# Reading two PSUM banks behind the sums that run beside them, and loading q further ahead in pieces

## The chip, the cores and the metric

The kernel runs on one core of one Trainium2 chip. The metric is the device time of one execution in microseconds (us), inputs and outputs in the chip's main memory. The span: first to last instruction; a kernel's trace is of one of its timed executions, that of the kernel before of a further one, of 982.29 us. The granted clock is the share of its full clock that the trace records for TensorE (PE in the profile): 1.00, or 0.5 in what is called half-clock stretches below. In this kernel TensorE multiplies matrices, VectorE (DVE) adds and multiplies elementwise, ScalarE (ACT) copies and does activations, SyncE (SP) issues transfers.

## The reference, cut to what matters

```python
def _attn_ref(q, k, v, g_norm):                    # (8, 8, 576, 64)
    kv = np.einsum('bhsd,bhse->bhde', k, v)
    out = np.einsum('bhsd,bhde->bhse', q, kv)
    rms = np.sqrt(np.mean(out * out, axis=-1, keepdims=True) + 1e-06)
    return out / rms * g_norm

def _moe_ref(x, w_in, w_out, s, b):                # x: 4608 x 512, w_in: 512 x 2048
    h = x @ w_in
    r = np.maximum(h, 0.0)
    g = s * (r * r) + b
    return g @ w_out                               # w_out: 2048 x 512
```

## The kernel before

The 4608 tokens are 36 chunks of 128, four chunks to a unit, so units 0 to 8. In each unit a first half computes h and g (`mm1`), a second half multiplies by w_out (`mm2`). Both replace eight products by seven and some sums (Strassen's scheme); from unit 2 on, five of the seven products with w_out are cut once more in the same way (`second_level`). So TensorE runs products while VectorE runs the sums for the products that come next. Attention for the next unit is mixed into the first half. In the trace of the kernel before, sums that were ready stood for 2.44 us behind a read that was not and that is written before them. So the order below sets here what waits for what.

The part of a second half (unit 2 and later) that the change touches:

```python
        def x5_of(j):                                   # the S1 T1 product
            st["x", j] = half(("x", j), "x")            # a PSUM bank
            product(5, j, st["x", j], True)             # 8 matmuls of 256 columns (16 in the profile)
            scaled(right("o2", j), st["x", j], b_21)    # VectorE reads the bank
        ...
            p2[5]()
            pump(2)                                     # two of w_out's tiles are loaded
            x5_of(0)
            s2((2, 3))                                  # sums in SBUF
            p6["sums"]((5, 6))
            p2[3]()
            p2[4]()
            pump(2)
            at(1)                                       # attention work, in unit 2 alone
            x5_of(1)
            p6["sums"]((7, 3))
            p7["sums"]((5, 6, 7))
            at(2)
            pump(2)
            p6[1]()                                     # product into the t bank, then VectorE reads it
            s4((0,))
            p6[2]()
            p6[6]()                                     # next product into the same t bank
```

The S1 T1 product is one of the seven, of a sum made from g and a sum made from w_out. `w_out`'s tiles stand in a ring of seven. The result of `x5_of`, in `right("o2", j)`, is not used until near the end of the unit. q is loaded two chunks at a time into one of two buffers, in short rows:

```python
            for h in range(H):
                for a in range(2):
                    rows = slice(32 * (2 * (h % 2) + a), 32 * (2 * (h % 2) + a) + 32)
                    nc.sync.dma_start(
                        out=to[rows, h // 2, w : w + n, :],
                        in_=src[h, :, j : j + n, a * 32 : a * 32 + 32],
                    )
```

That is 16 transfers for each run of positions of one batch. Most pairs of chunks are one such run; some are two (32 transfers) and one is three (48).

## Time and profile before

| | before |
|---|---|
| time of 3 runs, median (range) | 986.51 us (984.99 to 988.79) |
| the profiled run | 982.29 us, span 980.5 us |
| TensorE busy | 945.9 us, 96% |
| TensorE waiting for VectorE's read of the t_ps bank | 16.5 us, in seven waits |
| half-clock stretches after those waits | 5, of 3.413 us each |
| mean granted clock | 0.990 |

An engine that is busy for 96% of the span leaves little to win by waiting less; the table's last two rows show that waiting can also cost clock: five of the seven waits were followed by 3.413 us at 0.50.

### The profile page before, as it was taken

To read this page: it belongs to the slowest core of one execution; us is meant where nothing else is said; L and a number is where in the kernel's file an instruction comes from. 1 tells how busy PE (TensorE), PEld (TensorE's weight loads), DVE (VectorE), ACT (ScalarE), POOL (GpSimd) and SP (SyncE) were. 2 spreads that over 40 slices of the span, in tenths; PEclk is the share of its full clock that TensorE was granted. 3 is DMA by queue.
4 is the path that set the end of the run, shared out by engine and by line. 5 is a ranking of instruction groups with operands and counts; after the bars stand their busy time and mean duration, and the time that the engine had idled before them with its cause. 6 is when DMAs were issued, how large, how long until landed. Compare 5 with 4: busy or idle time off the path is not lost.

```text
span 980.5 us, 17772 instructions
## 1 busy us (share of the span) xinstructions
PE 945.9 (96%) x7270; PEld 846.2 (86%) x7270; DVE 641.9 (65%) x1167; ACT 192.8 (20%) x366; POOL 6.7 (1%) x18
## 2 busy tenths in 40 slices
PE   7999999999999899999999999999999999999997
PEld 6888888888888898889879888988898988898987
DVE  2789666584467666766477756766676667664674
ACT  3683132102121023200320023101320022001100
POOL 2000000000000000000000000000000000000000
PEclk9999999999999999999999999999999999999999
DMA  9679736497653546155445554355435530553054
GB/s 247 216 282 260 251 80 176 131 297 232 182 121 119 194 133 193 41 194 171 140 110 171 187 177 110 121 194 172 120 90 195 187 99 18 196 170 123 25 200 140
DMA packets 136656, 158.46 MB, mean 162 GB/s; under 512 B 77696, under 2 KB 91776, under 8 KB 136448
## 3 DMA queue, kind: packets, MB, share of 16 engines
q1 hardware_dynamic: 133472, 155.57, 52.3%
q10 hardware_dynamic: 2784, 1.77, 0.8%
q8 instruction: 57, 0.93, 0.4%
q14 instruction: 23, 0.19, 0.1%
q0 software_dynamic: 320, 0.00, 0.0%
HBM read 131.34 MB, written 25.95 MB: 160 GB/s over the span
## 4 chain that ended last, share of the span: by engine, by line
PE 87%; DVE 5%; DMA 4%; ACT 2%; SPq 1%; issue 1%; DVEq 0%; ACTq 0%
PE x_ps L91 39%; PE y_ps L91 26%; PE z_ps L91 9%; PE t_ps L91 8%; PE x_ps L434 3%; DVE sub L245 2%; PE kv_ps L372 2%; DMA w_sb<-w 1%; SPq L167 1%; DMA w_raw<-in_moe_w_in_dram 1%; DMA kv_sb<-in_k_dram 1%; ACT xT L484 1%; DVE o L697 1%; DVE sub L242 0%; DVE xT L478 0%
## 5 line engine op out<-in xcount | busy, mean ns | idle before, releaser
L582 ACT COPY r<-x_ps 128x512 f32<-128x512 f32 x96 | 56.3, 586 | 435.3 <-PE x_ps L91 393.6
L91 PE MATMUL y_ps<-xs,wb 128*128 128x256 f32 x512 | 122.7, 382 | 0.0
L91 PE MATMUL x_ps<-xs,ws 128*128 128x256 f32 x512 | 121.5, 380 | 0.0
L91 PEld LDWEIGHTS x_ps<-xs,ws 128*128 128x128 f32 x512 | 96.9, 190 | 14.0 <-issue 1.0
L91 PEld LDWEIGHTS y_ps<-xs,wb 128*128 128x128 f32 x512 | 95.3, 190 | 14.6 <-issue 2.2
L91 PE MATMUL x_ps<-xT,wa 128*128 128x256 f32 x384 | 90.3, 381 | 0.1
L242 DVE TENSOR_TENSOR a<-y_ps,r 128x512 f32<-128x512 f32 x64 | 44.1, 689 | 66.8 <-ACT r L582 61.9
L91 PEld LDWEIGHTS x_ps<-xT,wa 128*128 128x128 f32 x384 | 71.8, 190 | 11.1 <-issue 1.2
L91 PE MATMUL x_ps<-w_sb,a 128*128 128x256 f32 (+1 forms) x376 | 79.7, 364 | 0.0
L91 PE MATMUL t_ps<-w_sb,sub 128*128 128x128 f32 x448 | 63.1, 302 | 16.5 <-DVE r L697 16.5
L91 PEld LDWEIGHTS t_ps<-w_sb,sub 128*128 128x128 f32 x448 | 60.4, 215 | 18.2 <-DVE r L697 17.8
L91 PEld LDWEIGHTS x_ps<-w_sb,a 128*128 128x128 f32 x376 | 66.9, 190 | 8.4 <-issue 0.6
L537 DVE SCALAR_TENSOR_TENSOR a<-a 128x512 f32<-128x512 f32 x96 | 66.4, 691 | 3.1
L91 PE MATMUL y_ps<-w_sb,sub 128*128 128x128 f32 x504 | 62.0, 275 | 0.0
L91 PE MATMUL x_ps<-xT,ws 128*128 128x256 f32 x256 | 60.9, 381 | 0.5
L91 PEld LDWEIGHTS y_ps<-w_sb,sub 128*128 128x128 f32 x504 | 60.2, 192 | 0.7
L91 PE MATMUL z_ps<-xT,wa 128*128 128x256 f32 x256 | 60.5, 379 | 0.0
L91 PE MATMUL x_ps<-w_sb,s 128*128 128x256 f32 x256 | 57.8, 380 | 0.0
L91 PEld LDWEIGHTS x_ps<-xT,ws 128*128 128x128 f32 x256 | 47.8, 190 | 8.2 <-ACT r L582 2.1
L91 PEld LDWEIGHTS z_ps<-xT,wa 128*128 128x128 f32 x256 | 48.6, 190 | 6.6
L91 PE MATMUL y_ps<-w_sb,a 128*128 128x128 f32 (+1 forms) x360 | 54.3, 300 | 0.0
L91 PEld LDWEIGHTS x_ps<-w_sb,s 128*128 128x128 f32 x256 | 47.5, 190 | 6.0 <-issue 0.2
(139 smaller groups left out, 1236.4 us busy)
## 6 DMA issues: line engine op xcount, KB each, us to landing
w_sb<-w SPq DMA_DIRECT2D x147, 512.0 KB, 4.6
w_sb<-w SPq DMA_DIRECT2D x35, 256.0 KB, 2.8
w_raw<-in_moe_w_in_dram SPq DMA_DIRECT2D x8, 1024.0 KB, 8.1
w_raw<-in_moe_w_out_dram SPq DMA_DIRECT2D x8, 1024.0 KB, 5.3
w_sb<-in_k_dram SPq DMA_DIRECT2D x48, 144.0 KB, 2.9
w_sb<-in_v_dram SPq DMA_DIRECT2D x48, 144.0 KB, 3.0
out_dram<-o SPq DMA_DIRECT2D x104, 64.0 KB, 2.4
w<-sub SPq DMA_DIRECT2D x20, 256.0 KB, 3.9
```

Of the source, the lines that this page charges most:

```text
L91: nc.tensor.matmul(o, lhsT=lhsT, rhs=rhs, start=start, stop=stop, skip_group_check=True)
L167: nc.sync.dma_start(out=to[rows, h // 2, w : w + n, :], in_=src[h, :, j : j + n, a * 32 : a * 32 + 32],)
L242: nc.vector.tensor_tensor(out=o, in0=a, in1=b, op=ALU.add)
L245: nc.vector.tensor_tensor(out=o, in0=a, in1=b, op=ALU.subtract)
L372: nc.tensor.matmul(ps[r][l * HB : l * HB + HB, i, :], lhsT=kv[l][rows, 0, j, :], rhs=kv[l][rows, 1, j, :], start=(j == 0), stop=(j == R - 1),)
L434: nc.tensor.matmul(ps[32 * p : 32 * p + 32, w, :], lhsT=st["qT"][:, p, 32 * w : 32 * w + 32], rhs=bd_kv[(b if w < 2 else b1) % 2][:, p, :] ...
L484: nc.scalar.activation(to[:, i], to[:, i], AF.Copy, scale=g_col[:, i : i + 1])
L537: nc.vector.scalar_tensor_tensor(t, t, 0.0, t, ALU.max, ALU.mult)
L582: nc.scalar.copy(st[name], src)
L697: nc.vector.scalar_tensor_tensor(o, ps, s_col, other, ALU.mult, ALU.add)
```

## The change

Two things. First, the reads of the two x_ps banks are put behind sums that are ready earlier, so that VectorE works while TensorE is at the product, and then reads. Second, q of a unit's second pair of chunks is issued one unit earlier, in eight pieces between w_out's tiles, in place of one run at a unit's start. The arithmetic is the same. The core of the diff (the moves of attention work inside unit 2 that follow from it, and unit 1's loads, are cut):

```diff
-        def x5_of(j):
+        def x5_of(j, *between):
             st["x", j] = half(("x", j), "x")
             product(5, j, st["x", j], True)
+            for fn in between:
+                fn()
             scaled(right("o2", j), st["x", j], b_21)
 ...
-            x5_of(0)
-            s2((2, 3))
-            p6["sums"]((5, 6))
+            at(("q", 2))
+            x5_of(0, lambda: s2((2, 3)), lambda: p6["sums"]((5, 6)))
             p2[3]()
             p2[4]()
             pump(2)
+            at(("q", 3))
             at(1)
-            x5_of(1)
-            p6["sums"]((7, 3))
-            p7["sums"]((5, 6, 7))
+            x5_of(1, lambda: p6["sums"]((7, 3)), lambda: p7["sums"]((5, 6, 7)))
 ...
+    def loads_in_parts(u, i, parts):
+        left = []
+        def part(n):
+            if n == 0 and u < U:
+                left.extend(load_q(4 * u + 2 * i))
+            k = -(-len(left) // (parts - n))
+            for load in left[:k]:
+                load()
+            del left[:k]
+        return [partial(part, n) for n in range(parts)]
 ...
+        for n, fn in enumerate(loads_in_parts(u + 2, 1, 8)):
+            second["q", n + 2] = [fn]
 ...
-            loads(u + 1, 0 if u < 3 else 1)
+            if u < 3:
+                loads(u + 1, u - 1)
```

More of the change, by code (lines that the diff above doesn't have):

```diff
@@ L158, in load_q @@
                 q_in[R] = t[:, DM:].rearrange("p (a w) -> p a w", a=NP)
+        rest = []
         for w, b, j, n in pieces:
@@ L166, in load_q @@
                     rows = slice(32 * (2 * (h % 2) + a), 32 * (2 * (h % 2) + a) + 32)
-                    nc.sync.dma_start(
-                        out=to[rows, h // 2, w : w + n, :],
-                        in_=src[h, :, j : j + n, a * 32 : a * 32 + 32],
+                    rest.append(
+                        partial(
+                            nc.sync.dma_start,
+                            out=to[rows, h // 2, w : w + n, :],
+                            in_=src[h, :, j : j + n, a * 32 : a * 32 + 32],
+                        )
                     )
+        return rest
     wide = moe_w_in.dtype != FP32
@@ L974, in rest @@
             pump(2)
+            at(("q", 0))
             step["x3"]()
@@ L980, in rest @@
             pump(2)
+            at(("q", 1))
             at(0)
@@ L996, in rest @@
             pump(2)
+            at(("q", 3))
             at(1)
-            x5_of(1)
-            p6["sums"]((7, 3))
-            p7["sums"]((5, 6, 7))
+            x5_of(1, lambda: p6["sums"]((7, 3)), lambda: p7["sums"]((5, 6, 7)))
             at(2)
             pump(2)
+            at(("q", 4))
             p6[1]()
@@ L1011, in rest @@
             pump(2)
+            at(("q", 5))
             st["r2"] = rp.tile([P, 2, HN], FP32, name="or2", tag="rb")
@@ L1017, in rest @@
             pump(2)
+            at(("q", 6))
             p7[2]()
@@ L1022, in rest @@
             pump(2)
+            at(("q", 7))
             at(3)
@@ L1030, in between @@
                 pump(2)
+                at(("q", 8))
                 p4[1]()
@@ L1043, in rest @@
             pump(4)
+            at(("q", 9))
             y4_of(0, 3)
@@ L1046, in rest @@
             pump(2)
+            at(("q", 10))
         return {"sums": p1["sums"], "rest": rest}
@@ L1182, in side_of @@
             }
+        if u == 1:
+            for n, fn in enumerate(loads_in_parts(3, 0, 8)):
+                side.setdefault(6 + n, []).append(fn)
         return side
@@ L1187, in loads @@
         if u < U:
-            load_q(4 * u + 2 * i)
+            for load in load_q(4 * u + 2 * i):
+                load()
[6 more added lines that the diff above has]
+            for load in left[:k]:
+                load()
+            del left[:k]
+        return [partial(part, n) for n in range(parts)]
     tile_at = {1: 3, 2: 4, 3: 5, 4: 6, 5: 7, 6: 8, 7: 9, 9: 10, 10: 11, 11: 12, 12: 13, 14: 14, 15: 15}
@@ L1221, in sides @@
             first[1, 2] = [lambda: kv_product(kv_due[u]), lambda: pump(NP)]
-        first.setdefault((1, 2), []).append(lambda: loads(*((u + 1, 1) if u < 3 else (u + 2, 0))))
+        place, half = ((1, 2), (u + 2, 0)) if u > 2 else (((1, 2), (2, 1)), ((2, 2), (4, 0)))[u - 1]
+        first.setdefault(place, []).append(lambda: loads(*half))
         if u == 1 or u + 1 == U:
@@ L1226, in sides @@
         for s in range(NS):
-            j = s if u > 2 else s - 2
+            j = s if u > 2 else s - 1
             if j >= 0:
@@ L1232, in sides @@
         if u == 2:
-            first[3, 1].append(lambda: loads(4, 0))
-            second = {
-                0: [turn[2], product[2]], 1: [norm[2]], 2: [turn_x[2], turn[3]],
-                3: [product[3]], 4: [norm[3], turn_x[3]],
-            }
+            second = {0: [turn[3], product[3]], 1: [norm[3]], 2: [turn_x[3]]}
+        for n, fn in enumerate(loads_in_parts(u + 2, 1, 8)):
+            second["q", n + 2] = [fn]
         second[5] = [lambda: [sums() for sums in x_sums(u + 1)]]
```

## The prediction

> **What bounds the kernel now.** I read the page first, then the waits of TensorE, then its stream of instructions around one wait, then the granted clock around all of them, and last the wait on q.
>
> The page says that TensorE is the bound, and which wait it has in the steady state:
>
> ```profile
> PE 945.9 (96%) x7270; PEld 846.2 (86%) x7270; DVE 641.9 (65%) x1167; ACT 192.8 (20%) x366; POOL 6.7 (1%) x18
> ...
> L91 PE MATMUL t_ps<-w_sb,sub 128*128 128x128 f32 x448 | 63.1, 302 | 16.5 <-DVE r L697 16.5
> ```
>
> TensorE is busy for 96% of the span, so only what it waits for, or runs slowly for, can be won without taking matmuls away. The view of waits, for TensorE alone, begins:
>
> ```profile
> PE t_ps L91 <- DVE r L697: 16.5, 7, 3.4
> PE x_ps L434 <- DVE qT L404: 4.4, 3, 2.3
> ```
>
> Seven waits for VectorE's read of t_ps, 16.5 us together, and three for a transposed q, 4.4 us together. Unit 0 and 1 do not run this part, units 2 to 8 do: seven units, one wait each (3.37 us in unit 2, 2.18 or 2.19 in the others). The stream of VectorE and TensorE around the wait of unit 3 shows its cause:
>
> ```profile
> 424.71 0.48 DVE L697 SCALAR_TENSOR_TENSOR o<-x_ps,s_col,b 128x256 f32<-128x256 f32 x1 [2.44 <-PE x_ps L91]
> ...
> 426.29 3.62 PE L91 MATMUL x_ps<-w_sb,s 128*128 128x256 f32 x16
> ...
> 429.95 0.48 DVE L697 SCALAR_TENSOR_TENSOR o<-x_ps,s_col,b 128x256 f32<-128x256 f32 x1 [1.58 <-PE x_ps L91]
> ...
> 432.88 0.68 DVE L245 TENSOR_TENSOR sub<-a 128x512 f32<-128x512 f32 x1
> 433.48 0.34 DVE L697 SCALAR_TENSOR_TENSOR r<-t_ps,s_col,o 128x128 f32<-128x128 f32 x1
> ...
> 433.88 4.57 PE L91 MATMUL t_ps<-w_sb,sub 128*128 128x128 f32 x24 [2.19 <-DVE r L697]
> ```
>
> The reads of the x_ps bank (o<-x_ps, the S1 T1 product) stand ahead of sums that do not need it. VectorE sits idle 2.44 and then 1.58 us for the two products to end, and does its sums afterwards. Five of them (430.35 to 433.48) stand between the second read and the read of t_ps, and TensorE's next product into t_ps may not start before that read.
>
> There is a second cost, which no wait shows: the 24 matmuls after the wait take 4.57 us in unit 3 and 2.94 in unit 4. A table of 12 us around each wait has the granted clock in the column after POOL (here units 3, 4, 5 and 8):
>
> ```profile
> 430.69:442.69 12.00, 9.81 (x73) 9.62 (x73) 8.07 (x18) 0.00 (x0) 0.00 (x0) 0.86 0.47 163
> 538.52:550.52 12.00, 9.82 (x87) 9.63 (x87) 8.41 (x19) 0.00 (x0) 0.00 (x0) 1.00 0.59 196
> 642.32:654.32 12.00, 9.82 (x73) 9.63 (x73) 8.06 (x18) 0.00 (x0) 0.00 (x0) 0.86 0.49 172
> ...
> 947.59:959.59 12.00, 9.82 (x88) 9.63 (x88) 8.40 (x19) 0.00 (x0) 0.00 (x0) 1.00 0.58 198
> ```
>
> Five of seven waits (units 2, 3, 5, 6 and 7) are followed by a stretch at half clock: 0.86 of 12 us is 3.4 us at one half. Last, the longest wait for q, in unit 4, in the chain that ended last:
>
> ```profile
> 490.75 1.61 DMA q_sb<-in_q_dram
> ...
> 492.54 0.72 DVE qT L404
> ...
> 493.39 1.08 PE x_ps L434 x32
> ```
>
> The q tile of that pair of chunks is cut into 48 transfers, which the sync queue issues in one run from 474.5 to 498.8 us; the 32nd lands at 492.36, VectorE transposes, TensorE has waited 2.34 us.
>
> [...] the starts of the slow stretches, 328.61, 434.43, 646.05, 751.87 and 854.27 us, lie whole multiples of 3.413 apart. [...] On that grid, windows with 2.05 to 2.19 us of waiting were followed by half clock, and windows with 1.46 us (unit 4) or 1.58 us (the q wait at 306 us) were not. So where a wait of 2.18 us falls on the grid decides whether it costs 1.65 us more.
> [...] ready sums stand behind a read that waits 2.44 us. [...] one issue takes the sync queue 0.44 us (median of 304), 48 take over 20.
>
> **The change, part by part.** No matmul, sum or byte is added or removed; order alone moves.
>
> (1) The first read of x_ps goes behind two s2 sums and two p6 sums, the second behind five sums. Replayed for unit 3 with the starts above (a sum takes 0.60 to 0.72 us start to start): VectorE is free at 422.2; four sums, 2.53 us, end at 424.7, when the first x_ps is ready (424.71 before as well); read until 425.1; the two y_ps reads wait for TensorE, the last is done at about 426.7; five sums, 3.13 us, end at about 429.9; x_ps is ready at 429.95, read until 430.35; t_ps's first product ends at 430.64, its read runs from 430.84 to about 431.15. TensorE asks for t_ps at about 431.6. The wait is gone, by a margin of some 0.4 us. Six units (3 to 8): 6 × 2.18 = 13.1 us.
> Unit 2 carries attention work too. Its replay: y_ps reads done at 318.95, the norm's two instructions 0.9, five sums 3.13, read 0.4, transpose of xn 0.63, so t_ps is read from about 324.0 to 324.3, and TensorE asks at 323.9. It keeps about 0.5 of 3.37 us: 2.9 saved. (It had another transpose of q there, 0.6 us, which the change moves to the first half.)
>
> (2) Without those waits there is no window with 2 us idle: five half-clock stretches go. Each costs 4.57 − 2.94 = 1.63 us (in unit 2, 1.33 + 0.34 = 1.67). 5 × 1.65 = 8.2 us.
>
> (3) q of the second half is issued in eight pieces during the previous unit's second half, up to 60 us ahead of use. The 2.34 us wait of unit 4 goes. The one at 306 us (1.58) stays: q had landed long before, its transpose stands behind VectorE's sums, and the new order keeps that place. The 0.46 and 0.54 us waits of earlier units stay.
>
> Sum: 13.1 + 2.9 + 8.2 + 2.3 = 26.5 us, or 2.7%.
>
> **The rivals.**
> - A wait takes the place of the one removed: the read of t_ps is still late because the sums end late, or the x_ps bank is freed late. Against it: the replay's margin is 0.4 us, and each x_ps bank is next written by a product some 15 us on. If a wait of about 1 us stayed in seven units, 7 us would come back: about 965.
> - The sync queue becomes the bound: q pieces sit in front of w_out's tiles, and TensorE waits for w_sb. For it: around unit 1's end the queue has hardly a pause from 225 to 254 us, and the change puts 28 issues of 0.48 us (13 us) in there. I replayed that queue issue by issue: it is 9 us late at 252 us, the first 16 transfers of unit 2's q are issued by 241, the other 16 by 263, and are wanted near 256 and 269. Nothing waits, but the second margin is only some 5 us. Against it in units 3 to 8: the queue spends most of the second half waiting for TensorE to free a slot, and a piece costs 0.9 us (2.6 in the unit with 48). A miss in unit 2 would cost up to 6 us and one slow stretch: about 965.
> - q was hidden anyway, and part (3) gives nothing: 2.3 us less, about 960.
> - The half-clock stretches stay, set off by other waits: 8 us less, about 966. Against it: the 1.58 us wait set none off.
>
> **Range and chances.** The profiled run took 982.3 us, the timed ones 985.0, 986.5 and 988.8. Taking 26.5 off gives 956 from the profiled run and 960 from the median. The timed runs' surplus may be more half-clock stretches (the three waits of over 2 us that tripped none in the profile would add 3 × 1.65 = 5 us), and those would go too. I choose 958. A miss of one rival brings 965; everything at once and all timed surplus gone, 953. So 952 to 966. Faster by over 2% means under 966.8: 0.86. Within 2%: 0.13. Slower needs a new wait of over 46 us, which nothing here suggests: 0.01.
>
> **What would show it.** Right: TensorE's waits for t_ps vanish in units 3 to 8 and fall to about 0.5 us in unit 2; VectorE's idle time of 2.44 and 1.58 us before the reads of x_ps falls to under 0.3; the granted clock is 1.00 in all seven stretches, with 24 t_ps matmuls at 2.94 us; the wait for q in unit 4 is gone and that of 1.58 us in unit 2 is still there; units 3 to 7 each take about 101.7 us. Wrong: a wait of TensorE for w_sb or q in unit 2, a t_ps wait of 1 us or more, slow stretches elsewhere. If the waits go and the time falls by less than 20 us, TensorE has found another wait that I did not name.

## More of the kernel before

One line that the prediction tells but does not show is the sync queue's stream in the first half of unit 4: start, duration, and the 48 issues for one pair of chunks between two lots of w_out's tiles.

```profile
474.54 24.23 SPq L167 DMA_DIRECT2D q_sb<-in_q_dram  x48
498.87 1.41 SPq L666 DMA_DIRECT2D w_sb<-w  x3
```

## The result, and the profile after

| | before | after |
|---|---|---|
| median of 6 runs (range) | 986.56 us (984.9 to 989.54) | 957.9 us (956.88 to 959.2) |
| ratio | | 0.9706, 95% interval 0.9687 to 0.9725 |
| the profiled run, span | 980.5 us | 955.3 us |
| mean granted clock, profiled run | 0.990 | 0.999 |
| t_ps waits of TensorE | 16.5 us, 7 | 0.4 us, 1 |
| waits for a transposed q | 4.4 us, 3 | 2.1 us, 2 |
| waits for w_out's tiles (w_sb) | none | 1.9 us, 2 |
| half-clock stretches, but for the kernel's end | 5 | 0 |

Ratios here are the mean time of one kernel's fast runs over that of the other's fast runs in the same rounds, so not quite the ratio of the medians. All outputs are right.

The page of the changed kernel, to be held against the two lines shown of before; the group of t_ps matmuls has gone from 302 ns each to 275, and from 16.5 us idle to 0.4:

```profile
PE 938.2 (98%) x7270; PEld 838.4 (88%) x7270; DVE 643.9 (67%) x1167; ACT 192.3 (20%) x366; POOL 6.7 (1%) x18
...
L91 PE MATMUL t_ps<-w_sb,sub 128*128 128x128 f32 x448 | 54.7, 275 | 0.4 <-DVE r L702 0.4
```

The waits of TensorE alone begin (us in total, times, longest):

```profile
PE x_ps L439 <- DVE qT L409: 2.1, 2, 1.6
PE x_ps L91 <- DMA w_sb<-w: 1.9, 2, 1.0
```

The second of these is new. VectorE's stream in unit 3, at the place shown of before:

```profile
419.93 0.69 DVE L250 TENSOR_TENSOR sub<-sub,a 128x512 f32<-128x512 f32 x1
420.54 0.48 DVE L702 SCALAR_TENSOR_TENSOR o<-x_ps,s_col,b 128x256 f32<-128x256 f32 x1
...
424.99 0.69 DVE L250 TENSOR_TENSOR sub<-a 128x512 f32<-128x512 f32 x1
425.65 0.48 DVE L702 SCALAR_TENSOR_TENSOR o<-x_ps,s_col,b 128x256 f32<-128x256 f32 x1
426.54 0.35 DVE L702 SCALAR_TENSOR_TENSOR r<-t_ps,s_col,o 128x128 f32<-128x128 f32 x1 [0.41 <-PE t_ps L91]
```

The reads of x_ps come straight after the sums, without the idle time of 2.44 and 1.58 us that stood in brackets before; now it is VectorE that waits for t_ps, 0.41 us, where TensorE waited for VectorE. And the clock, in 12 us around the same place in units 2 and 3:

```profile
322.88:334.88 12.00, 11.58 (x101) 11.31 (x100) 8.13 (x19) 1.71 (x4) 0.00 (x0) 1.00 0.84 258
424.29:436.29 12.00, 12.00 (x104) 11.85 (x103) 7.51 (x18) 0.00 (x0) 0.00 (x0) 1.00 0.67 205
```

1.00 in the column after POOL, and TensorE is busy for 11.58 and 12.00 of 12 us, where it was busy for 8.63 and 9.81 before. The new wait, in unit 3, in the chain that ended last:

```profile
434.25 0.42 SPq L1217
...
434.77 4.24 DMA w_sb<-w
439.00 0.04 issue
439.05 1.99 PE x_ps L91 x8
```

Unit 3 loads the pair of chunks with 48 transfers, six to a piece. The tile of w_out is issued after one such piece and lands 4.24 us later, just too late for TensorE (0.99 us). Its place in the ring was free when TensorE ended a t_ps product, at 431.86, 2.9 us before the issue. In the kernel before and in order_only the queue waits for that place, and issues this tile 0.03 us after that product in all seven units. Unit 5, whose pair has 32 transfers, has the other such wait (0.91), at the same tile:

```profile
634.07 2.55 SPq L1217 DMA_DIRECT2D q_sb<-in_q_dram  x4
636.72 0.39 SPq L674 DMA_DIRECT2D w_sb<-w  x1
```

Here the place was free at 635.82, so the issue is only 0.9 us late; but this tile takes 6.17 us to land, where the median of such tiles from unit 3 on is 4.7 in this trace. With the delay or the slow landing alone, TensorE would hardly have waited. Whether the q transfers under way slow the landing is not shown: in the kernel before, too, some tiles took over 6 us.

The sum for the two profiled runs: t_ps waits 16.5 − 0.4 = 16.1 us, half-clock stretches 5 × 1.65 = 8.2, q waits 2.3, w_sb waits −1.9, together 24.7 us; the spans differ by 25.2.

### The profile page after: what moved, and what is told of

It is laid out like the page before.

```text
span 955.3 us, 17799 instructions
## 1 busy us (share of the span) xinstructions
PE 938.2 (98%) x7270; PEld 838.4 (88%) x7270; DVE 643.9 (67%) x1167; ACT 192.3 (20%) x366; POOL 6.7 (1%) x18
## 4 chain that ended last, share of the span: by engine, by line
PE 88%; DMA 5%; DVE 3%; ACT 2%; issue 1%; SPq 1%; ACTq 0%; DVEq 0%
PE x_ps L91 40%; PE y_ps L91 26%; PE z_ps L91 9%; PE t_ps L91 7%; PE x_ps L439 3%; DMA w_sb<-w 2%; PE kv_ps L377 2%; DMA w_raw<-in_moe_w_in_dram 1%; DMA kv_sb<-in_k_dram 1%; ACT xT L489 1%; DVE sub L250 1%; DVE xn L458 1%; DVE xT L483 1%; ACT bd_kv L392 0%; DMA w<-w_sb 0%
## 5 line engine op out<-in xcount | busy, mean ns | idle before, releaser
L91 PE MATMUL t_ps<-w_sb,sub 128*128 128x128 f32 x448 | 54.7, 275 | 0.4 <-DVE r L702 0.4
L91 PEld LDWEIGHTS t_ps<-w_sb,sub 128*128 128x128 f32 x448 | 52.8, 192 | 1.0 <-DVE r L702 0.6
```

What stands on the lines that cost most here:

```text
L91: nc.tensor.matmul(o, lhsT=lhsT, rhs=rhs, start=start, stop=stop, skip_group_check=True)
```

## The experiments

Twelve kernels ran, in four lots on four chips, each lot beside the kernel before. The medians of the kernel before in them were 986.42, 986.58, 984.69 and 985.16 us, so a difference of 1 us between lots says little.

### Each part alone

**order_only**: the kernel before with the reads moved (`x5_of` as in the change), q loaded as before and attention work not moved.

```diff
-            x5_of(0)
-            s2((2, 3))
-            p6["sums"]((5, 6))
+            x5_of(0, lambda: s2((2, 3)), lambda: p6["sums"]((5, 6)))
 ...
-            x5_of(1)
-            p6["sums"]((7, 3))
-            p7["sums"]((5, 6, 7))
+            x5_of(1, lambda: p6["sums"]((7, 3)), lambda: p7["sums"]((5, 6, 7)))
```

> The reads of x_ps moved behind the sums, q loaded as in the kernel before. My theory (the order carries nearly all: 13.1 us of waits in units 3 to 8, 2.3 in unit 2, 8.2 of half clock): 962 to 965 us; TensorE's waits for t_ps are 0 in units 3 to 8 and about 1 us in unit 2 (it keeps a second transpose of q in front of the read); the wait of 2.3 us for q in unit 4 stays; no wait of TensorE for w_sb, since the queue issues no q between w_out's tiles. Rival (the early q carries a large part, by keeping the sync queue free): over 970.

Measured: 961.97 us (960.09 to 963.36), ratio 0.9762 [0.9732, 0.9792]. The t_ps wait is 1.01 us in unit 2 and none elsewhere, and there is no wait for w_sb. The expected time holds, at its lower end. But the wait for q in unit 4 did not stay at 2.3 us. TensorE's waits have it as the longest of this line:

```profile
PE x_ps L434 <- DVE qT L404: 5.8, 3, 3.8
```

TensorE now comes to that point 8.2 us earlier than it did (482.88 for 491.06 us), the q that it needs lands only 6.7 us earlier: the wait grows from 2.34 to 3.81 us, and the trace has one half-clock stretch in the middle of this kernel, right behind it.

**loads_only**: the changed kernel with the two reads back where they were.

```diff
-            x5_of(0, lambda: s2((2, 3)), lambda: p6["sums"]((5, 6)))
+            x5_of(0)
+            s2((2, 3))
+            p6["sums"]((5, 6))
 ...
-            x5_of(1, lambda: p6["sums"]((7, 3)), lambda: p7["sums"]((5, 6, 7)))
+            x5_of(1)
+            p6["sums"]((7, 3))
+            p7["sums"]((5, 6, 7))
```

> q loaded early and in pieces, reads of x_ps left where they were. My theory: the 2.3 us wait in unit 4 goes, the t_ps waits (2.2 us, seven times) and the half-clock stretches stay, so 982 to 986, within 0.5% of the kernel before. If the two waits for w_sb of 0.9 us in units 3 and 5 come from q pieces delaying tiles that TensorE reaches 4 us earlier than before, they are gone or smaller here. Rival (early q carries a large part): under 976.

Measured: 980.85 us (980.59 to 982.95), ratio 0.996 [0.993, 0.9989]: 1.2 us under the expected range by its median; by its ratio within the expected 0.5% of the kernel before. The q wait of unit 4 is gone; the seven t_ps waits stay (15.9 us) and so do four half-clock stretches. The w_sb waits of units 3 and 5 are gone, but the trace has two others, of 0.39 us in unit 6 and 1.00 in unit 8, and in unit 8 no piece of q is issued any more. So small waits for w_sb come and go, and q is not behind each of them.

So the order carries most of the gain, and the early q is worth little alone. After the order, it is worth more: from 961.97 to 957.9 us by the medians, in two lots, and 3.0 us by the spans of the two traces (958.3 and 955.3).

### Which of the two reads

**first_only** moves the first read alone, **second_only** the second alone (each is the changed kernel with one of the two lines of the diff above taken back).

> The changed kernel with only the first of the two reads moved (the second stands ahead of the five sums again). My replay: TensorE's wait is set by the five sums between the second read and the read of t_ps, which are all still there, so the wait is 2.2 us again in units 3 to 8 and half-clock stretches return: 981 to 986. Rival (each read's move earns its own idle time, 2.44 us for the first): about 968.

> The changed kernel with only the second read moved. Replay: VectorE idles 2.4 us before the first read again, so it comes 1 us late to the five sums: a t_ps wait of about 0.6 us in units 3 to 8, about 1.9 in unit 2, no slow stretch: 957.9 + 3.6 + 1.5 = about 963 us (961 to 965). Rival (the second move alone is enough): 957 to 959.

Measured: first_only 980.95 us (978.0 to 982.55), ratio 0.9952 [0.9913, 0.9991]; second_only 962.43 us (960.99 to 962.73), ratio 0.9761 [0.9739, 0.9783]; both as expected (first_only 0.05 us below its range). TensorE's t_ps waits, of first_only and then of second_only:

```profile
PE t_ps L91 <- DVE r L702: 15.9, 7, 2.8
```

```profile
PE t_ps L91 <- DVE r L702: 5.0, 7, 1.9
```

The first move alone brings nothing, the same 15.9 us as in loads_only: VectorE's idle time only moves from before the first read to before the second (3.10 us there in unit 3), and the five sums between the second read and that of t_ps are all still there. The second alone brings all but 0.51 us in units 3 to 8 and 1.94 in unit 2 (replayed: 0.6 and 1.9). What counts is not how long VectorE idles but what stands between the late read and the read that TensorE waits for.

### How much waiting costs, and when it costs clock

**three_behind** and **four_behind**: three or four of the five sums behind the second read again.

```diff
 # three_behind
-            x5_of(1, lambda: p6["sums"]((7, 3)), lambda: p7["sums"]((5, 6, 7)))
+            x5_of(1, lambda: p6["sums"]((7, 3)))
+            p7["sums"]((5, 6, 7))
 # four_behind
-            x5_of(1, lambda: p6["sums"]((7, 3)), lambda: p7["sums"]((5, 6, 7)))
+            x5_of(1, lambda: p6["sums"]((7,)))
+            p6["sums"]((3,))
+            p7["sums"]((5, 6, 7))
```

> The changed kernel with three of the five sums behind the second read again. Replay: t_ps is read 1.93 us after x_ps, TensorE waits about 1.07 us in units 3 to 8 and about 1.6 in unit 2 (0.4 now), no slow stretch as no window reaches 2 us: 957.9 + 6 x 1.07 + 1.15 = about 965.5 us (964 to 967). Rival (any wait at this place trips the clock): six or seven slow stretches more, 974 or over.

> Four of the five sums behind the second read. Replay: waits of about 1.67 us in units 3 to 8 and about 2.2 in unit 2. If the threshold is 2 us in a window: 957.9 + 6 x 1.67 + 1.75 = about 969.7 us with at most one slow stretch (968 to 972). If the threshold lies between 1.6 and 1.67: up to seven stretches of 1.65 us, 974 to 981.

Measured: three_behind 964.29 us (963.27 to 966.38), ratio 0.9786 [0.9765, 0.9807]; four_behind 970.64 us (969.13 to 971.18), ratio 0.9845 [0.9826, 0.9864]. Both inside the expected range. The waits are 0.98 us (unit 2: 1.57) and 1.59 us (unit 2: 2.18). Of four_behind, 12 us around the waits of units 2 and 3:

```profile
325.67:337.67 12.00, 9.82 (x73) 9.63 (x73) 8.06 (x18) 1.71 (x4) 0.00 (x0) 0.86 0.59 177
431.09:443.09 12.00, 10.41 (x91) 10.20 (x91) 8.00 (x19) 0.00 (x0) 0.00 (x0) 1.00 0.64 183
```

Within one kernel, the wait of 2.18 us is followed by half clock and the one of 1.59 us is not, nor are the five others of 1.59. With all runs at this place in one table:

| sums behind the second read | kernel | t_ps waits in all | half-clock stretches at them | median |
|---|---|---|---|---|
| 0 | changed kernel | 0.4 us | 0 | 957.9 us |
| 0, first read not moved | second_only | 5.0 | 0 | 962.43 |
| 3 | three_behind | 7.5 | 0 | 964.29 |
| 4 | four_behind | 11.7 | 1 | 970.64 |
| 5 | first_only | 15.9 | 5 | 980.95 |

Up to 7.5 us of waiting, a microsecond of it costs about a microsecond of time. From 11.7 to 15.9 us, 4.2 us more of waiting cost 10.3 us; the waiting itself and four more stretches at 1.65 us each make 10.8. (The first row is of another lot than the next three, the last of a third.)

How long were the t_ps waits that half clock followed, in units 2 to 8? None of up to 1.94 us was among them; the longest of these are 1.94 us in second_only, 1.6 in filled (below), six of 1.59 in four_behind and 1.57 in three_behind. Of the waits of 2.18 us and more, half clock followed five of seven in the kernel before, five of seven in first_only, four of seven in loads_only and the one in four_behind. So a wait of 2.18 us can be followed by it or not, and the trace of the kernel before allows an estimate of what decides: its five stretches start at 328.61, 434.43, 646.05, 751.87 and 854.27 us, the later four 31, 93, 124 and 154 times 3.413 us after the first, to 0.05 us. Cut at lines of that spacing, the five waits that were followed by half clock have 2.05 to 2.19 us between two lines; the two that were not, in units 4 and 8, lie across a line and have at most 1.46 and 1.25 us. That the place on these lines decides is no more than an estimate from this one trace.

**filled**: the kernel before, with eight useless matmuls (16 in the profile) in each wait. It multiplies the identity into a bank that nobody reads.

```diff
+        def fill(n):
+            ps = bank_of("fill", "y")
+            for _ in range(n):
+                matmul(ps[:, 0, :P], ident, ident, True, True)
 ...
             p6[2]()
+            fill(8)
             p6[6]()
```

> The kernel before with eight matmuls of no use (1.8 us) put into each t_ps wait, writing a bank that nobody reads. TensorE does more and waits less, but gets nothing done earlier. Theory of the clock (half clock follows a window with about 2 us of waiting, and costs 1.65 us each): no slow stretches, 975 to 980 us. Rival (slow stretches have another cause[...]): same time as before or up to a few us more, 985 to 989.

Measured: 976.6 us (975.83 to 979.28), ratio 0.9917 [0.9886, 0.9948]. TensorE's stream in unit 3:

```profile
430.12 1.06 PE L91 MATMUL z_ps<-w_sb,a 128*128 128x128 f32 x8
431.01 1.95 PE L91 MATMUL y_ps<-ident 128*128 128x128 f32 x16
433.36 2.94 PE L91 MATMUL t_ps<-w_sb,sub 128*128 128x128 f32 x24 [0.40 <-DVE r L697]
```

The product into t_ps still starts when VectorE has read the bank, no earlier. But its 24 matmuls take 2.94 us, not 4.57, and the same kernel with more work takes 9.8 us less (976.6 for 986.42). The seven waits are 1.6 us at most, and none is followed by half clock. (One place is: the q wait of unit 4, here 3.58 us long, with a half-clock stretch of 6.83 us that begins in it.) So with more work and less idle time of TensorE the half clock behind these waits goes, and its cost (4.57 − 2.94 = 1.63 us in unit 3) is separate from that of the wait.

### The pieces of q, and what they do to w_out's tiles

**burst**: the changed kernel, with each second pair's q in one run between w_out's tiles.

```diff
-        for n, fn in enumerate(loads_in_parts(u + 2, 1, 8)):
+        for n, fn in enumerate(loads_in_parts(u + 2, 1, 1)):
```

> The changed kernel, with the q of each unit's second half issued in one run between w_out's tiles, not in eight pieces. If pieces matter: in unit 3 (48 issues, 21 us of the sync queue) w_out's tiles come late and TensorE waits about 10 us for w_sb, in unit 5 (32 issues, 14 us) a few us; units with 16 (7 us) stay without a wait since seven tiles stand ready (12.5 us of matmuls): 968 to 975. If the queue has room anyway: 957 to 960.

Measured: 995.04 us (991.78 to 996.54), ratio 1.0091 [1.0065, 1.0116]: slower than the kernel before, and 20 us over the top of what I expected. The sync queue in unit 3, and TensorE beside it:

```profile
417.65 23.79 SPq L1217 DMA_DIRECT2D q_sb<-in_q_dram  x48
```

```profile
428.42 2.84 PE L91 MATMUL t_ps<-w_sb,sub 128*128 128x128 f32 x24
445.87 2.08 PE L91 MATMUL y_ps<-w_sb,a 128*128 128x128 f32 x8 [14.61 <-DMA w_sb<-w]
```

48 issues hold the queue for 23.79 us. TensorE goes on from the tiles that it has until 431, then waits 14.6 us. The units with 32 transfers, 4 and 5, wait 7.9 us each, and half-clock stretches of 17.1, 10.2 and 10.2 us accompany these waits, partly while TensorE stands still and partly after it; the eight matmuls after the wait take 2.08 us, twice the 1.06 of elsewhere. I had sized the wait alone and forgotten the clock behind it, and had missed unit 4. That the load is in pieces is thus needed for the gain: early, but in one run at this place, would lose more than all of it.

**act_queue**: the pieces are issued by ACT, which has little to do in a second half (the diff leaves out that `load_q` takes the queue as `whole`). **act_queue_later** adds product_later (next) to it.

```diff
-                left.extend(load_q(4 * u + 2 * i))
+                left.extend(load_q(4 * u + 2 * i, whole=nc.sync if i == 0 else nc.scalar))
```

> The changed kernel with the q pieces of the second halves issued by the ACT queue, which has 1 to 2 us of work in a second half, instead of the sync queue. Theory (the two waits for w_sb in units 3 and 5, 1.9 us together, come from q issues standing in front of w_out's tiles on the sync queue): both waits go, 956.0 us (955 to 957). Rival (the small q packets slow the tiles on the way, whoever issues them, or the waits of ACT hold up its copies): no gain, 957.5 or more.

> Both of the above in one: 954.4 us (953.5 to 956) if the two gains are separate.

Measured: act_queue 965.46 us (961.98 to 968.6), ratio 0.9795 [0.9762, 0.9827]; act_queue_later 964.0 us (960.88 to 965.55), ratio 0.9775 [0.9748, 0.9801]. Both are some 9.5 us over the expected time: my theory fell in this form. TensorE's waits for w_sb in act_queue have grown to 6.3 us, in units 3, 4 and 5, where the tile shown above is issued 4.7, 1.2 and 2.3 us after its place was free, and two of the three are followed by a half-clock stretch. By the traces that is 4.4 + 2 × 1.65 = 7.7 of the 9.5 us between the two spans; another 1.6 stand in the first 40 us, where this trace, like five others, has a half-clock stretch that the changed kernel's has not. The sync queue's own waits in unit 3's second half, second and third in length, tell what holds the tiles:

```profile
SPq L671 <- DMA q_sb<-in_q_dram: 15.3, 7, 5.1
SPq L674 <- DMA q_sb<-in_q_dram: 6.3, 2, 5.2
```

The issues of w_out's tiles wait 21.6 us for q transfers to land, though these are on another queue: the two queues did not free each other here. What ties an issue to the transfers of the other queue was not shown. Whether the packets of q also slow the tiles on the way is left open by this run.

**product_later**: in unit 2, the product that reads the transposed q goes one place behind the transpose.

```diff
-            second = {0: [turn[3], product[3]], 1: [norm[3]], 2: [turn_x[3]]}
+            second = {0: [turn[3]], 1: [product[3]], 2: [norm[3]], 3: [turn_x[3]]}
```

> The changed kernel; in unit 2's second half the product that reads the transposed q is moved one place later than the transpose. Theory: the 1.59 us wait that is left in unit 2 comes from TensorE reaching that product before VectorE has passed its sums and the transpose; it goes to about zero, 956.3 us (955.5 to 957.2). Rival (the delay moves to the norm and on to the read of t_ps in that unit): same as the changed kernel, 957.9.

Measured: 955.06 us (954.68 to 956.43), ratio 0.9692 [0.9666, 0.9718]. The wait of 1.59 us is gone from the trace, and the t_ps wait of that unit is 0.62 in place of 0.42 us. The time is 0.4 us under the expected range. The median is lower than that of the changed kernel by 2.8 us, but on another chip, and the intervals of the two ratios overlap: that the wait goes is shown, the gain in time is not clear of noise.

**fewer_issues**: product_later, with q in fewer transfers, over ten places from unit 3 on.

```diff
+            for m in range(n if n < 4 else 0):          # a run of 2: 8 transfers, not 16
+                for l in range(2):
+                    for a in range(2):
+                        rows = slice(32 * (2 * l + a), 32 * (2 * l + a) + 32)
+                        rest.append(partial(
+                            nc.sync.dma_start, out=to[rows, :, w + m, :],
+                            in_=src[l::2, :, j + m, a * 32 : a * 32 + 32].rearrange("h t d -> t h d")))
-            for h in range(H):
+            for h in range(H if n >= 4 else 0):
 ...
-        for n, fn in enumerate(loads_in_parts(u + 2, 1, 8)):
-            second["q", n + 2] = [fn]
+        early = 2 if u == 2 else 0
+        for n, fn in enumerate(loads_in_parts(u + 2, 1, 10 - early)):
+            second["q", n + early] = [fn]
```

> The version with the product of unit 2 one place later, and the q of the second halves in fewer transfers (a stretch of two positions takes 8 instead of 16, so unit 3 has 32 instead of 48 and unit 5 has 24 instead of 32), spread over ten places instead of eight from unit 3 on: at most 4 issues between two pairs of w_out's tiles. Theory (what delays the tiles is the number of q transfers between them[...]): TensorE's waits for w_sb in units 3 and 5 go, 953.5 to 955 us, the best of all. Rival (the q bytes on the way slow the tiles, however few the issues): waits of about 0.9 us stay, 955 to 956.5.

Measured: 954.68 us (954.14 to 955.82), ratio 0.9699 [0.9674, 0.9724]; span 952.7 us, the shortest of all. TensorE no longer waits for w_sb at all: of its waits of over 0.3 us, those left after the kernel's first 40 us are 0.54 and 0.47 us for attention work in units 0 and 1, and 0.62 us for t_ps in unit 2. It also issues the tile shown above 0.03 us after its place is free in all seven units, where product_later, with the pieces of the changed kernel, is 2.64, 0.41 and 0.49 us late in units 3 to 5. So the q issues between the tiles are what delayed it. How much TensorE waits for the delay depends on the landing too: product_later waits 0.70 us in unit 3 and not in unit 5, and the waits of loads_only in units 6 and 8 follow issues that are in time. The run changes the places of the pieces as well as the number of transfers, so it does not separate the two. In time it is the same as product_later within the noise. Both beat the changed kernel by their medians, neither beyond doubt.

## Why the prediction was right

The time was 957.9 us for 958 predicted. That it is met to 0.1 us is luck: 958 was chosen between 956 and 960, the sum of 26.5 us stands against 25.2 between the traces and 28.7 between the medians, and part 3 had errors that cancel. By its own steps:

- **Part 1, the waits for t_ps.** Predicted 13.1 + 2.9 = 16.0 us, measured 16.1 (16.5 to 0.4). In units 3 to 8 they are gone; unit 2 keeps 0.42 us for some 0.5 predicted. order_only shows that the new order does it without the loads, and first_only and second_only that the mechanism is the one told: sums between the second read and that of t_ps.
- **Part 2, the half clock.** Predicted 8.2 us from five stretches. All five are gone, and 24 t_ps matmuls take 2.84 us in unit 3 (2.94 predicted). filled, with the seven waits at 1.6 us or less, has none behind them.
- **The surplus of the timed runs.** The prediction guessed that the three other runs of the kernel before were slower than the profiled one because of more such stretches. Each run's mean granted clock is on record. Of 36 runs of the kernel before, the 16 with a clock of 0.990 or more have a median of 983.7 us, the 10 with 0.987 or less one of 987.0. The six runs of the changed kernel have 0.997 to 1.000. That agrees with the guess: 28.7 us by the medians, 25.2 by the profiles.
- **Part 3, q.** This is the term that was mis-sized, with a right sum by two errors that partly cancel. Predicted: 2.3 us won, nothing lost. In order_only the wait that the loads take away is 3.81 us, not 2.34, with a half-clock stretch behind it (about 1.65), and unit 2 waits 0.6 us longer for t_ps; that is 6.1 us to win. Lost are 1.9 us of new waits for w_sb. The net would be 4.2 us. The medians of order_only and the changed kernel differ by 4.1, but in two lots; the two traces that the sum is made from differ by 3.0. Of the missing 1.2 us, 0.4 lie in the first 25 us, before any change acts; the rest was not traced. I had read the wait's length from a kernel in which TensorE came later, and had added parts that are not independent. The 1.58 us wait of unit 2 stayed, as predicted (1.59).
- **The rivals.** That t_ps would be read late again, no. That the sync queue would hold up w_out's tiles: in part, and not where I looked. At the end of unit 1, q's 32nd transfer was issued at 269.1 us, 6 us later than in my replay, and its transpose at 273.3 did not wait for it. In units 3 and 5, where I wrote that the queue had time, TensorE waited 1.9 us in all: in unit 3 q's issues delayed a tile by 2.9 us, in unit 5 by 0.9, and there it also took 6.17 us to land. burst shows how much worse this can be.
- **Its signs.** VectorE's idle time before the reads of x_ps is gone, as foretold. That units 3 to 7 take about 101.7 us each was too simple: from the t_ps product of one unit to that of the next it is 102.6, 101.4, 102.5, 98.5 and 93.4 us, starting with unit 3.
- **One reading to narrow.** The prediction sets the 0.44 us of one issue beside the more than 20 of 48. Beside the transfer, one issue is short: 0.44 us for 1.7 to 3.0 us from issue to landing (medians by size, in the kernel before). A run of 48 is not: it held the queue for 24.23 us there.

## What to carry to other kernels

When an engine takes its work in order, as VectorE did here (ready sums stood for 2.44 us behind a read), put a read that must wait for a product behind all work that is ready before it, and count what stands between that read and the next one that someone else waits for; here that count was the gain (the second read's move alone took the t_ps waits from 15.9 to 5.0 us, the first's alone left them at 15.9), not the idle time. Keep TensorE's waits short where waiting costs clock: here a wait of 2.18 us could cost another 1.65, none of the six of 1.59 did, and useless matmuls in the wait paid (976.6 us for 986.42). A load that is early enough still has to be cut so that its issues do not stand for long in front of a transfer that is needed soon (in burst, 23.79 us of issues made TensorE wait 14.6 us), and its worth should be sized in the kernel with the other changes in it.
